# First lanes from the second group on, linear part on the last tile, VectorE scales the last two groups, a new order table

## Chip, cores and metric

The kernel runs on one core of a Trainium2 chip. The metric is the device time of one execution in microseconds. The kernel before takes 559.15 us (median of three runs, 559.07 to 559.81).

## The reference

Attention over 32 inducing points, twice, and then a feed-forward block with a PReLU:

```
B, N, C = 4, 12480, 128        # x
m = 32                         # inducing points
def mab(q, kv):
    a = softmax(scale * q @ kv.T)
    return a @ kv
h = mab(I, x)                  # per batch: 32 x 128
y = mab(x, h)                  # 12480 x 128 per batch
h1 = y @ w_in                  # 49920 x 2048
g = max(h1, 0) + alpha * min(h1, 0)
out = g @ w_out                # 49920 x 128, float32
```

## The kernel before

**What is computed per group.** Tokens are taken in groups of 512. A batch has 25 groups: six super-tiles of four groups and one last group of 192 tokens; groups are written (batch, number), so (0,0) to (3,24). The second attention has only 32 keys, so its product with `w_in` is folded into one small matrix per batch: hW = h @ w_in, 32 x 2048 (`h_weights`). Unnormalized softmax weights of a super-tile are computed (`b_scores`), go through DRAM (`e2d`) and come back four times below each other as `rep`, so that every 32-row strip of the tensor array finds a copy. A group then takes 16 *fills*: a matmul with 32 contraction rows (`hW` x `rep`) on one of the four 32-row strips, into a bank of PSUM, from where ACT or DVE writes relu to a `gt` tile in SBUF (`fill`, L596; ACT L614 or DVE L617). PReLU is relu times (1 - alpha) plus a linear part: the relu part goes through W1 = (1 - alpha) w_out, the linear part is one matmul with the small matrix hA (`linear`, one strip; `linear_whole` with a quarter of hA on all rows), which needs Amat (`w_amat`, 16 matmuls once) and `h_linear`. The sum of a group is transposed by DVE (`ot`, L664), scaled by the softmax denominators (`ob`, POOL, L667) and written out by four DMAs (`finish`, L653).

**Two ways to sum a group.** In the *whole* way the 16 gt tiles are contracted over all 128 rows, one matmul each (`whole`). In the *lanes* a gt tile is contracted in four strip matmuls of 32 rows. The first strip does its 16 for a group, hands the group to the second, and so on to the fourth; the four strips work on four different groups at once, each adding to its own bank, while fills go on whichever strip is free. A bank must not be written by two strips at a time: at a hand-over the next strip waits on a semaphore (`fence`), which is raised by a PE drain (`hand_over`, L966 to L974). Where the instruction before can carry the semaphore the drain vanishes in the built program; the others stand alone (L969, 19 of them before).

**The order.** `tokens` writes down PE's order by hand with a planner's clock: the lane loop chooses the next fill, piece, start, enter, warm or spare matmul by its model of when banks and tiles come free. `PLAN` has a letter for each laned group that sets four knobs (how hungry ACT and DVE must be, room, cost of a fill, whether to hand over at once). Other work (scores of later super-tiles, the next batch's first attention, transposes) is put into `tasks` at numbered steps; a step that touches PE in another shape is a pause, at which the lanes stop for a whole-array stage. The order of the engines' instructions is fixed (`pin`).

**Phases.** A prologue makes h of batch 0. Then SESSIONS (8) sessions do groups (0,0) and (0,1) the whole way: four fills, tasks, four whole matmuls of the session before. Then come the lanes for 92 groups, from a first `start` (step T0 = 9); the last group of each batch, and the groups (3,22) and (3,23), go the whole way, the last three in the tail. While strips 2 and 3 have nothing in the first lanes, *warm* matmuls on W1 go there (`fresh`), and *spare* ones at the end. The `gt` pool has KEPT = 62 tiles. `rep` tiles come from a pool of three; the part of the first super-tile that PE makes directly (`rep0`, L522) takes one of the three.

**DMA queues.** POOL's queue issues loads of x (`a_load`) and most output; SP's issues e2d, rep, rt, rdT and the transposes; the last four groups' outputs go by SP and ACT, and two of group (3,23) wait in `late` until the end (POOL, L688).

The lines that start a lane are these:

```
tile[0] = [queue.pop(0), [None] + list(range(KC))]
...
t = max(free_at[f], seen[ch][1] - 100 - SLOT)
```

None stands for the linear part.

Of the kernel before, what the change touches and what calls it, by code (L numbers as in the profile page):

```python
# [17 lines left out]
P = 128  # L18
NB = 4
GRP = P * NB  # L20
NQ = 4
# [3 lines left out]
TAIL = 2  # L25
AHEAD = 8
LAND = 8000
KEPT = 62
RDS = 4
# [8 lines left out]
PLAN = (  # L38
    "aaKKfGcyLqmADMamiiznjafamQcyaqcafqanqaxacmOaav"
    "AmnCamKeacfymraaJmRnAynqyauaNmmgadjmafycQazyAm"  # L40
)
# [3 lines left out]
def kernel(  # L45
# [476 lines left out]
    def b_scores_pe(st, q):  # L522
        if q == 0:
            st.rep0 = rep_pool.tile([P, NQ, GRP], bf16, name="rep", tag="rep")
        ps = bank()
        mm(ps[:], st.hT4[:], tokens_of(st, 0, q))
        pin(nc.scalar.activation(
            out=st.rep0[:, q, :].rearrange("p (t j i) -> p t j i", j=NB, i=32),
            in_=turned(ps[:], NB), func=EXP, scale=scale_of(st),
        ))  # L530
        drained(ps, "A", 490, 240)
        st.rep[q] = st.rep0[:, q, :]
# [120 lines left out]
    def finish(b, g):  # L653
        st = states[b]
        pp, nb, _ = shape_of(g)
        t = pp * nb
        acc = acc_of(b, g)
        s, q = divmod(g, NQ)
        rq = st.rden[s][:, :, :, q : q + 1]
        rbc = bass.AP(  # L660
            tensor=rq.tensor, offset=rq.offset, ap=[rq.ap[0], rq.ap[1], rq.ap[2], [0, 32]]
        )
        ot = ot_pool.tile([P, GRP], f32, name="ot", tag="ot")
        pin(nc.vector.transpose(out=ot[:, :t], in_=acc[:, :t]))  # L664
        drained(accs[b, g], "D", 74 + t * 1.04)
        ob = ob_pool.tile([P, GRP], f32, name="ob", tag="ob")
        pin(nc.gpsimd.tensor_tensor(  # L667
            out=ob[:, :t].rearrange("p (k m c) -> p k m c", k=nb, c=32),
            in0=ot[:, :t].rearrange("p (k m c) -> p k m c", k=nb, c=32),
            in1=rbc, op=MULT,  # L670
        ))
        t0 = b * N + s * SUP
        if s < NS:
            dst = out[t0 : t0 + SUP, :].rearrange(
                "(i b q) (a k) -> q a i b k", b=t // 32, q=NQ, k=32)[q]
        else:
            dst = out[t0 : t0 + REM, :].rearrange("(i b) (a k) -> a i b k", b=t // 32, k=32)
        ending = b == B - 1 and g >= NG - 4
        for a in range(4):
            eng = (nc.sync, nc.scalar)[a % 2] if ending and g >= NG - 3 else nc.sync if ending else nc.gpsimd  # L680
            src = ob[32 * a : 32 * a + 32, :t].rearrange("p (b k) -> p b k", k=32)
            if b == B - 1 and g == NG - 2 and a > 1:
                late.append((dst[a], src))
            else:
                pin(eng.dma_start(out=dst[a], in_=src))  # L685
        if b == B - 1 and g == NG - 1:
            for dst, src in late:
                pin(nc.gpsimd.dma_start(out=dst, in_=src))  # L688
        st.rep.pop(g)
# [132 lines left out]
    def tokens(st):  # L822
# [15 lines left out]
        tail = [y for y in direct[2:] if y[0] == B - 1]  # L838
        tail.sort()
# [3 lines left out]
        need = [ch for _, ch in sorted(need)]  # L843
        SESSIONS = 8
        T0 = SESSIONS + 1

# [13 lines left out]
        at(4, lambda: b_turn(st, 0))  # L860
        at(5, w_amat)
        at(6, lambda: h_linear(st))
        for b in range(B):
            base = T0 + (first[b, 0] if b else -2)
            for s in range(1, NS + 1):
                t = base + 4 * s - AHEAD - (b == 0 and s > 4) if b or s > 2 else 4 * s - 2
                nt = t + (5 if b == 0 and s == 2 else 3 if b == 0 and s == 4 else 4 if s < NS or b + 1 < B else 2)
# [4 lines left out]
            if b + 1 < B:  # L872
# [7 lines left out]
                else:  # L880
                    score = [T0 + k for k in (2, 4, 4, 6, 9, 11, 13)]
                    load = [0, 0, 5, SESSIONS, T0 + 2, T0 + 4, T0 + 6]
                    cross = [None, None, 6, T0 + 1, T0 + 4, T0 + 7, T0 + 8]
                    at(7, lambda: p_xpose(states[1], 0, 0))
                    at(SESSIONS, lambda: p_xpose(states[1], 0, 1))
                    at(T0 + 2, lambda: p_xpose(states[1], 1, 0))
                    at(T0 + 3, lambda: p_xpose(states[1], 1, 1))
                sums = [T0 + k for k in (4, 6, 6, 9, 11, 13, 14)] if n == 1 else [k + 4 for k in score]
                fs, fa = (t_scores, t_accum) if n == 1 else (a_scores, a_accum)
# [31 lines left out]
        for t in range(SESSIONS):  # L921
# [32 lines left out]
        assert len(plans) == len(laned)  # L954
        fresh = {f: bank() for f in (2, 3)}

# [19 lines left out]
        while queue or moving or owed or any(tile):  # L976
            best = []
            taken = {q for _, q, _ in moving} | {f + 1 for _, f in owed}
            for f in range(4):
                if tile[f]:  # L980
                    y, todo = tile[f]
                    if todo[0] is None:
                        best.append((free_at[f], 0, f, "linear"))
                    elif (*y, todo[0]) in seen:
                        t = max(free_at[f], seen[*y, todo[0]][1] - 100)
                        best.append((t, 1, f, "piece"))
                else:
# [4 lines left out]
                    if f == 0 and queue and lanes < LANES and (  # L992
# [3 lines left out]
                        if ch in seen:  # L996
                            t = max(free_at[f], seen[ch][1] - 100 - SLOT)
                            best.append((t, 2, f, "start"))
            if fillable():
                since = max(min(clk.free[i] for i in idle) - 40, landed.get(need[0][:2], 0))  # L1000
                hungry = min(clk.act, clk.dve) < clk.pe + hungry_at
                for f in range(4):
# [3 lines left out]
                    elif not tile[f]:  # L1006
                        best.append((t, 4 + (f in taken), f, "fill"))
            soon = min(max(x[0], clk.pe) for x in best) < clk.pe + 2 * SLOT
            for f in sorted(fresh):
# [7 lines left out]
            calm += [x for x in best if x[3] in ("warm", "spare")]  # L1017
            if owed and not best:
                hand_over()
                continue  # L1020
            if owed and not calm and at_once:
# [16 lines left out]
            if what == "start":  # L1038
# [11 lines left out]
                else:  # L1050
                    run_tasks(T0 + m)
                tile[0] = [queue.pop(0), [None] + list(range(KC))]
                continue
            if what == "enter":
                x = next(x for x in moving if x[1] == f)
                moving.remove(x)
                tile[f] = [x[0], list(range(KC))]
                gate[f] = fences[x[0], f]
# [16 lines left out]
            else:  # L1075
# [4 lines left out]
                else:  # L1080
# [5 lines left out]
                    if f == 3:  # L1086
                        seen.pop(ch)
                    if not todo:
                        tile[f] = None
                        if f < 3:  # L1090
                            owed.append((y, f))
                        flush()
            free_at[f] = clk.pe + SLOT
# [51 lines left out]
```

## Time and profile before

| | us |
|---|---|
| median of three runs | 559.15 |
| the profiled execution | 558.86 |
| its span, first to last instruction | 557.1 |
| first fills of the sessions | from 25.38 |
| lanes, with whole-array stages between | 41.66 to 541.68 |
| last three groups, whole | 541.68 to 550.59 |
| last output DMA issued on POOL | 552.27 |

The largest groups of instructions, with count, busy time, mean duration in ns of one and, after the second bar, idle time before them and what ended it:

```profile
L138 PE MATMUL bank<-gt,W 32*128 32x512 bf16 (+1 forms) x6013 | 482.9, 374 | 1.6 <-DVE gt L617 0.3
L614 ACT ACTIVATE gt<-bank 128x512 bf16<-128x512 f32 (+1 forms) x923 | 467.9, 620 | 14.3 <-PE bank L138 10.2
L617 DVE TENSOR_SCALAR gt<-bank 128x512 bf16<-128x512 f32 (+1 forms) x645 | 403.7, 676 | 19.9 <-PE bank L138 16.4
L667 POOL TENSOR_TENSOR ob<-ot,rdT 128x512 f32<-128x512 f32 (+1 forms) x100 | 111.0, 1110 | 93.5 <-DVE ot L664 83.7
```

Busy times of matmuls overlap: four strips work at once, so a mean of 374 ns each is not 374 ns of time. ACT's and DVE's instructions follow each other more closely than their means say: 467.9 us for 923 are 0.51 us each, 403.7 for 645 are 0.63. Granted TensorE clock was 0.998 over the span.

### The profile page before, as it was taken

The numbers are of one execution on the slowest core, as the hardware profiler recorded it, in microseconds if no ns is written. First come the engines' busy times: TensorE is split into PE (matmuls) and PEld (weight loads), VectorE is DVE, ScalarE is ACT, GpSimd is POOL, SyncE is SP. The second block draws the span as 40 slices with busy tenths as digits, with TensorE's granted clock in tenths as the row PEclk, the third lists the DMA queues.
The fourth block names the chain that finished last, engine by engine and source line by source line (L and its number), as shares of the span: only waits on it lengthen the run. The fifth ranks groups of instructions, "written<-read, shape, count | busy, mean of one in ns | idle before, by whom it ended". The sixth has DMA issues, their size and how long they took to land.

```text
span 557.1 us, 21434 instructions
## 1 busy us (share of the span) xinstructions
PE 538.6 (97%) x8890; PEld 293.1 (53%) x8894; DVE 497.3 (89%) x858; ACT 503.8 (90%) x1008; POOL 411.4 (74%) x602
## 2 busy tenths in 40 slices
PE   4999999999999999999999999999999999999995
PEld 4645555555455555544555556554465554454642
DVE  3689999989999999999998999999998999999981
ACT  2479999999989999999999999999999999999980
POOL 6556466967898978878698878665668859767683
PEclk9999999999999999999999999999999999999999
DMA  9976999645999998687577996333334334333224
GB/s 196 230 136 142 134 192 176 132 94 89 151 199 165 176 144 164 148 120 150 102 131 131 169 170 140 64 93 88 75 81 112 73 81 118 65 94 65 47 62 75
DMA packets 110209, 69.25 MB, mean 124 GB/s; under 512 B 78800, under 2 KB 100672, under 8 KB 110112
## 3 DMA queue, kind: packets, MB, share of 16 engines
q0 software_dynamic: 23344, 38.66, 37.6%
q1 hardware_dynamic: 84624, 28.46, 26.3%
q8 instruction: 69, 1.13, 0.9%
q10 hardware_dynamic: 2144, 0.77, 0.5%
q14 instruction: 28, 0.23, 0.2%
HBM read 41.00 MB, written 28.95 MB: 126 GB/s over the span
## 4 chain that ended last, share of the span: by engine, by line
PE 31%; issue 27%; PEld 25%; POOL 8%; DMA 4%; ACT 3%; DVE 1%; PEldq 1%; POOLq 0%; DVEq 0%
PE bank L138 31%; PEld L138 25%; POOL out_dram L685 5%; DMA xn<-in_x_dram 3%; POOL ob L667 3%; ACT gt L614 2%; PEldq L969 1%; PE bank L226 1%; DMA out_dram<-ob 1%; DVE gt L617 1%; DVE hW L313 0%; POOL xn L180 0%; DVE ot L664 0%; DMA rt<-rd 0%; PEld bank L138 0%
## 5 line engine op out<-in xcount | busy, mean ns | idle before, releaser
L138 PE MATMUL bank<-gt,W 32*128 32x512 bf16 (+1 forms) x6013 | 482.9, 374 | 1.6 <-DVE gt L617 0.3
L614 ACT ACTIVATE gt<-bank 128x512 bf16<-128x512 f32 (+1 forms) x923 | 467.9, 620 | 14.3 <-PE bank L138 10.2
L617 DVE TENSOR_SCALAR gt<-bank 128x512 bf16<-128x512 f32 (+1 forms) x645 | 403.7, 676 | 19.9 <-PE bank L138 16.4
L138 PE MATMUL bank<-rep,hW 32*128 32x512 bf16 (+1 forms) x1600 | 417.9, 368 | 2.0 <-DVE hW L313 0.3
L138 PEld LDWEIGHTS <-W 32*128 32x128 bf16 (+1 forms) x6109 | 229.1, 92 | 188.0 <-issue 117.2
L685 POOL DMA_DIRECT2D out_dram<-ob x384 | 247.0, 673 | 36.9 <-POOL ob L667 27.8
L667 POOL TENSOR_TENSOR ob<-ot,rdT 128x512 f32<-128x512 f32 (+1 forms) x100 | 111.0, 1110 | 93.5 <-DVE ot L664 83.7
L138 PEld LDWEIGHTS <-hW 32*128 32x128 bf16 x1600 | 135.6, 91 | 31.3 <-issue 15.1
L664 DVE STREAM_TRANSPOSE ot<-bank 128x512 f32<-128x512 f32 (+1 forms) x100 | 69.7, 697 | 16.3 <-PE bank L138 15.0
L180 POOL DMA_DIRECT2D xn<-in_x_dram x70 | 40.4, 656 | 3.6 <-DMA xn<-in_x_dram 2.4
L138 PE MATMUL bank<-rep,hA 32*128 32x512 bf16 x94 | 35.0, 376 | 0.3 <-DVE hW L313 0.2
L232 DVE COPY xT<-bank 128x1024 bf16<-128x1024 bf16 (+1 forms) x16 | 10.8, 672 | 5.1 <-PE bank L226 4.9
L138 PE MATMUL bank<-W 32*128 32x512 bf16 x93 | 13.8, 376 | 0.0
L253 ACT ACTIVATE e1t<-bank 128x256 bf16<-128x256 f32 (+1 forms) x13 | 4.8, 372 | 9.7 <-PE bank L138 9.5
L138 PEld LDWEIGHTS <-hA 32*128 32x128 bf16 x94 | 8.5, 91 | 7.3 <-issue 4.8
L226 PE MATMUL bank<-ident,xn 128*128 128x128 bf16 x128 | 11.3, 242 | 0.9 <-DVE xn L786 0.9
L138 PE MATMUL bank<-xT,hT 128*32 128x512 bf16 (+1 forms) x98 | 10.4, 389 | 0.6 <-ACT gt L614 0.4
L498 ACT ACTIVATE e<-bank,rs 128x512 bf16<-128x512 f32 x12 | 8.4, 699 | 2.5 <-PE bank L138 2.3
L226 PEld LDWEIGHTS <-xn 128*128 128x128 bf16 x128 | 8.7, 109 | 2.2 <-DVE xn L786 1.0
L498 ACT ACTIVATE e<-bank 128x512 bf16<-128x512 f32 x12 | 7.4, 616 | 2.4 <-PE bank L138 2.4
L138 PE MATMUL bank<-IT,xT 128*128 128x32 bf16 x192 | 8.0, 179 | 0.2
L138 PEld LDWEIGHTS <-hT 128*32 128x32 bf16 (+1 forms) x122 | 5.0, 93 | 5.8 <-issue 4.0
(103 smaller groups left out, 144.4 us busy)
## 6 DMA issues: line engine op xcount, KB each, us to landing
out_dram<-ob POOLq DMA_DIRECT2D x374, 64.0 KB, 2.9
rep<-e2d SPq DMA_DIRECT2D x92, 128.0 KB, 3.3
xn<-in_x_dram POOLq DMA_DIRECT2D x48, 128.0 KB, 5.5
xn<-in_x_dram POOLq DMA_DIRECT2D x22, 256.0 KB, 6.9
e2d<-e SPq DMA_DIRECT2D x24, 128.0 KB, 3.1
rdT<-rt SPq DMA_DIRECT2D x96, 8.0 KB, 2.4
w_out_f<-in_moe_w_out_dram POOLq DMA_DIRECT2D x4, 256.0 KB, 11.2
xs<-in_x_dram SPq DMA_DIRECT2D x1, 512.0 KB, 4.8
```

Of the source, the lines that this page charges most:

```text
L138: return pin(nc.tensor.matmul(o, lhsT, rhs, start=start, stop=stop, **kw))
L180: pin(nc.gpsimd.dma_start(out=xn[:, i * w : (i + 1) * w, :], in_=src[:, i * w : (i + 1) * w, :]))
L226: pin(nc.tensor.transpose(tp[:, k * P : (k + 1) * P], xn[:, q, j * C : (j + 1) * C], ident[:]))
L232: pin(nc.vector.tensor_copy(out=dst, in_=tp[:, :w]))
L253: pin(nc.scalar.activation(out=e1t[:pp, :nb, :].rearrange("p k m -> p (k m)"), in_=ps[:pp, : nb * M], func=EXP, scale=scale,))
L498: pin(nc.scalar.activation(out=e2[:].rearrange("p (t j i) -> p t j i", j=n, i=32), in_=turned(ps[:pp, :w], n), func=EXP, scale=scale_of(st ...
L614: pin(nc.scalar.activation(out=gt[:, :w], in_=ps[:, :w], func=RELU))
L617: pin(nc.vector.tensor_relu(gt[:, :w], ps[:, :w]))
L664: pin(nc.vector.transpose(out=ot[:, :t], in_=acc[:, :t]))
L667: pin(nc.gpsimd.tensor_tensor(out=ob[:, :t].rearrange("p (k m c) -> p k m c", k=nb, c=32), in0=ot[:, :t].rearrange("p (k m c) -> p k m c", ...
L685: pin(eng.dma_start(out=dst[a], in_=src))
L969: pin(nc.tensor.drain(fusable=True)).then_inc(fence, 1)
```

## The change

Groups: SESSIONS goes from 8 to 4, and only (0,0) is summed the whole way at the start; (0,1) becomes the first laned group, 93 in all. Amat, h_linear and the linear part of (0,0) become stages at the first three steps of the lanes; the scores of super-tile 2 come at step 4 in place of 6, and the steps of batch 1's first attention move with T0 (5 in place of 9) and by one or two more. The linear part stands behind the 16 pieces on strip 3 in place of before them on strip 0, and is offered only once hA is there. Warm matmuls are only for strip 3. `rep0` gets its own tile of two groups; `gt` has two tiles less. The last two groups' scaling is on DVE. PLAN is another table, with one letter more.

```
-KEPT = 62
+KEPT = 60
 PLAN = (
-    "aaKKfGcyLqmADMamiiznjafamQcyaqcafqanqaxacmOaav"
-    "AmnCamKeacfymraaJmRnAynqyauaNmmgadjmafycQazyAm"
+    "aaLCMLqymRymyimmKyalcavyVacyvMdiamfyafGcjamDcy"
+    "xyKnKymeqazGaaneialaMjaMFaMjccjommQamlcclccKya"
+    "a"
 )
...
-            st.rep0 = rep_pool.tile([P, NQ, GRP], bf16, name="rep", tag="rep")
+            st.rep0 = const.tile([P, 2, GRP], bf16, name="rep0")
...
-        pin(nc.gpsimd.tensor_tensor(
+        eng = nc.vector if b == B - 1 and g >= NG - 2 else nc.gpsimd
+        pin(eng.tensor_tensor(
...
-        direct = every[:2] + [(b, NG - 1) for b in range(B)] + every[-1 - TAIL : -1]
+        direct = every[:1] + [(b, NG - 1) for b in range(B)] + every[-1 - TAIL : -1]
...
-        SESSIONS = 8
+        SESSIONS = 4
...
-        at(5, w_amat)
-        at(6, lambda: h_linear(st))
+        at(T0, w_amat)
+        at(T0 + 1, lambda: h_linear(st))
+        at(T0 + 2, lambda: (linear_whole(0, 0), flush()))
...
-            base = T0 + (first[b, 0] if b else -2)
+            base = T0 + (first[b, 0] if b else -1)
...
-                t = base + 4 * s - AHEAD - (b == 0 and s > 4) if b or s > 2 else 4 * s - 2
+                t = base + 4 * s - AHEAD - (b == 0 and s > 4) if b or s > 2 else 2 * s
...
-                    score = [T0 + k for k in (2, 4, 4, 6, 9, 11, 13)]
-                    load = [0, 0, 5, SESSIONS, T0 + 2, T0 + 4, T0 + 6]
-                    cross = [None, None, 6, T0 + 1, T0 + 4, T0 + 7, T0 + 8]
+                    score = [T0 + k for k in (3, 5, 5, 7, 10, 12, 14)]
+                    load = [0, 0, SESSIONS, T0 + 1, T0 + 3, T0 + 5, T0 + 7]
+                    cross = [None, None, T0 + 1, T0 + 2, T0 + 5, T0 + 8, T0 + 9]
...
-        for f in range(2):
-            linear(0, f, f)
...
-        finish(*held.pop(0))
         run_tasks(SESSIONS)
-        flush()
...
-        fresh = {f: bank() for f in (2, 3)}
+        fresh = {3: bank()}
...
-                        best.append((free_at[f], 0, f, "linear"))
+                        if hasattr(states[y[0]], "hA"):
+                            best.append((free_at[f], 0, f, "linear"))
...
-                            t = max(free_at[f], seen[ch][1] - 100 - SLOT)
+                            t = max(free_at[f], seen[ch][1] - 100)
...
-                tile[0] = [queue.pop(0), [None] + list(range(KC))]
+                tile[0] = [queue.pop(0), list(range(KC))]
...
-                tile[f] = [x[0], list(range(KC))]
+                tile[f] = [x[0], list(range(KC)) + [None] * (f == 3)]
```

In the built programs the change moves these counts: whole matmuls on W1 128 to 112, strip matmuls on W1 and gt 5888 to 5952, warm and spare matmuls 93 to 61, standalone drains 19 to 26, evictions by ACT 923 to 927 (of these 18 of 384 columns in place of 20), by DVE 645 to 641.

More of the change, by code (lines that the diff above doesn't have):

```diff
@@ L837, in tokens @@
                 wholes[c + 1].append((b, NG - 1, u))
-        tail = [y for y in direct[2:] if y[0] == B - 1]
+        tail = [y for y in direct[1:] if y[0] == B - 1]
         tail.sort()
@@ L880, in tokens @@
                 else:
-                    score = [T0 + k for k in (2, 4, 4, 6, 9, 11, 13)]
-                    load = [0, 0, 5, SESSIONS, T0 + 2, T0 + 4, T0 + 6]
-                    cross = [None, None, 6, T0 + 1, T0 + 4, T0 + 7, T0 + 8]
[L884 to L888, printed above, removed]
+                    score = [T0 + k for k in (3, 5, 5, 7, 10, 12, 14)]
+                    load = [0, 0, SESSIONS, T0 + 1, T0 + 3, T0 + 5, T0 + 7]
+                    cross = [None, None, T0 + 1, T0 + 2, T0 + 5, T0 + 8, T0 + 9]
+                    at(T0 + 1, lambda: p_xpose(states[1], 0, 0))
+                    at(T0 + 2, lambda: p_xpose(states[1], 0, 1))
+                    at(T0 + 3, lambda: p_xpose(states[1], 1, 0))
+                    at(T0 + 4, lambda: p_xpose(states[1], 1, 1))
+                sums = [T0 + k for k in (5, 7, 7, 10, 12, 14, 15)] if n == 1 else [k + 4 for k in score]
                 fs, fa = (t_scores, t_accum) if n == 1 else (a_scores, a_accum)
@@ L1007, in tokens @@
                         best.append((t, 4 + (f in taken), f, "fill"))
+            if owed and not best:
+                hand_over()
+                continue
             soon = min(max(x[0], clk.pe) for x in best) < clk.pe + 2 * SLOT
@@ L1017, in tokens @@
             calm += [x for x in best if x[3] in ("warm", "spare")]
-            if owed and not best:
-                hand_over()
-                continue
             if owed and not calm and at_once:
@@ L1087, in tokens @@
                         seen.pop(ch)
[L1088 to L1092, printed above, removed]
+                if not todo:
+                    tile[f] = None
+                    if f < 3:
+                        owed.append((y, f))
+                    flush()
             free_at[f] = clk.pe + SLOT
```

## Prediction

> **What bounds the kernel now.** I read the page first, then the windows by stage, then PE's timeline where the lanes begin and every engine's timeline at the end.
>
> ```profile
> span 557.1 us, 21434 instructions
> PE 538.6 (97%) x8890; PEld 293.1 (53%) x8894; DVE 497.3 (89%) x858; ACT 503.8 (90%) x1008; POOL 411.4 (74%) x602
> ...
> PE 31%; issue 27%; PEld 25%; POOL 8%; DMA 4%; ACT 3%; DVE 1%; PEldq 1%; POOLq 0%; DVEq 0%
> ```
>
> The chain of waits is 83% TensorE in its three forms. ACT and DVE are no bystanders, though, as the windows show (per stage: PE, PEld, DVE, ACT, POOL busy, clock, DMA share, GB/s):
>
> ```profile
> 33.73:41.66 7.93, 7.44 (x74) 3.83 (x72) 6.69 (x15) 5.03 (x9) 1.59 (x4) 1.00 1.01 170
> 41.66:75.79 34.13, 34.13 (x575) 18.20 (x573) 31.54 (x53) 32.26 (x65) 20.54 (x29) 1.00 0.88 154
> 75.79:300.00 224.21, 222.53 (x3819) 119.69 (x3819) 208.92 (x364) 215.83 (x437) 178.87 (x258) 1.00 0.80 142
> ...
> 541.68:550.60 8.92, 8.86 (x52) 4.68 (x51) 2.15 (x3) 0.00 (x0) 4.69 (x7) 1.00 0.49 88
> ```
>
> In the lanes (row three) ACT is 96% and DVE 93% busy: TensorE and the two evicting engines are nearly in balance, so neither can gain much there alone. The first row is the last part of the sessions: there ACT is 63% and DVE 84% busy. That is the one stage before the tail in which all three engines have slack, and the change takes it out.
>
> PE's timeline there (start, duration, tiles, count):
>
> ```profile
> 32.66 0.81 PE L138 MATMUL bank<-gt,W 128*128 128x512 bf16 x3 [0.16 <-issue]
> 33.40 0.39 PE L138 MATMUL bank<-rep,hW 32*128 32x512 bf16 x4
> 33.73 1.07 PE L138 MATMUL bank<-AW,winT 128*128 128x128 bf16 x16
> 34.63 1.03 PE L138 MATMUL bank<-gt,W 128*128 128x512 bf16 x4
> 35.59 0.39 PE L138 MATMUL bank<-rep,hW 32*128 32x512 bf16 x4
> ...
> 41.66 0.39 PE L138 MATMUL bank<-rep,hW 32*128 32x512 bf16 x2
> 41.67 0.39 PE L138 MATMUL bank<-W 32*128 32x512 bf16 x2
> ```
>
> Four fills, then four whole matmuls, with switches between: from 33.40 on, 8.26 us for 16 fills. The lanes begin at 41.66.
>
> The unit of the rest: a *round* is one 32-row matmul of 512 columns on a strip; in a stretch between two whole-array stages the fullest strip counts the rounds. I counted each stretch's matmuls in the order of the built program and took its time from PE's timeline. The 33 stretches from 41.66 to 541.68 have 1965 rounds in 464.2 us: **0.2362 us a round**. By work (all strips' matmuls over four: 1899) it is 0.2444. The whole-array stages between take the other 35.8 us. A whole matmul costs 0.216 (the tail's run of 15 takes 3.40 us, the last alone about 0.38).
>
> **The change part by part.** *Counts that cancel.* Group (0,1) leaves the whole array: 16 whole matmuls fewer (3.46 us), 64 strip matmuls more. 32 warm or spare matmuls go (93 to 61). Evictions stay at 1568; a net 4 move from DVE to ACT. I cost these through the rounds below, not twice.
>
> *The start.* The built program after the change keeps fills and whole matmuls as they are up to the fifth block of fills at 32.11. Then come the whole matmuls (to 33.40), the scores of super-tile 2 moved up (0.33 from start to next start, as at 36.66 to 36.99 here), four fills (0.33), and the Amat product, which the first lane waits for (0.90, from 33.73 to 34.63). Lanes start at 33.40 + 0.33 + 0.33 + 0.90 and a switch of some 0.15: **35.1**. What the cut sessions held moves into the lanes: up to the stage with the rest of batch 1's accumulations, which opens at 75.79 before, the new order has 145 rounds in place of 130, and five whole-array stages in place of three. Rounds at this region's own pace: the 130 took 31.1 us, 0.239 each, so 145 take 34.7. Stages from their parts: the stage at 51.92 took 1.46 (pick, scores, transposes, IT products); pick and transposes alone are 0.64, with Amat's product 0.71; the one at 57.96 (transposes) took 0.55, with the whole linear 0.77; the other three 1.28, 0.64 and 1.03; sum 4.4. So the common point comes at 35.1 + 34.7 + 4.4 = 74.2 against 75.79, with 142 fills issued against 140 and one piece fewer. Two added drains (none before) may take 0.1 of it. **-1.5 us.** Bounds: at the quickest stretch's 0.221 a round the 145 cost 2.6 less (-4.1); at 0.245, the slowest here, 0.8 more, and if evictions hold the first lane by a further 1 us, the end is +0.3.
>
> *Common point to the end of lanes.* The same stages; 1839 rounds against 1835, by work 1777.0 against 1775.75. Standalone drains (L969): 24 more against 19, which is 5 more. By work +1.25 x 0.2444 = +0.3; by rounds +0.9. A drain lasts 0.55 us (median of 19) against 0.24 for the round it displaces, so 5 cost up to 1.6 if nothing else was late; a fit over the 33 stretches gives 0.06 to 0.12 each, because evictions catch up meanwhile and the next rounds run closer. I take **+0.3**, by work, since three engines share the bound here; the other end is +0.9 + 1.6 = +2.5. The fit misses a stretch by 0.28 us, over 29 stretches 1.5 us: so it may also be -1.2.
>
> *Linear part on the last tile.* 92 strip matmuls change from strip 0 to strip 3, one becomes a whole one (0.22 in place of 0.06); contained in the rounds. A group's transposition starts one matmul (0.22) later, and its bank was taken one later too. Nothing is queued behind but the next group's.
>
> *Queues and buffers.* SP: the e2d and rep transfers of super-tile 2 (5 DMAs) pass the rt, xTr and rdT transfers of super-tile 1; POOL: two xn loads pass the first ob. SP would hold rt by a landing of e2d, 3.1 us median; rdT's readers are covered, since POOL waits for DVE's ot in 83.7 us of its idle time and for rdT once (9.7). Two gt buffers less: the program's stock peaks at 59 in place of 61 and lies at 45 to 58 for most of the run. Nothing for either; without that cover a fill waits one eviction, 0.6.
>
> *The end.*
>
> ```profile
> 549.33 0.72 DVE L664 STREAM_TRANSPOSE ot<-bank 128x512 f32<-128x512 f32 x1 [2.95 <-PE bank L138]
> 550.13 1.55 POOL L667 TENSOR_TENSOR ob<-ot,rdT 128x512 f32<-128x512 f32 x2 [2.59 <-DVE ot L664]
> 550.70 0.38 DVE L664 STREAM_TRANSPOSE ot<-bank 128x192 f32<-128x192 f32 x1 [0.66 <-PE bank L138]
> 551.62 1.29 POOL L688 DMA_DIRECT2D out_dram<-ob  x2
> ```
>
> DVE has no two-tensor row of 128x512 in SBUF. Nearest: its TENSOR_SCALAR of 128x512, 0.68; its TENSOR_TENSOR of 128x128, 0.29; POOL's 1.08 as upper end. With 0.68, ob of group 23 is done at 550.8 (551.2 on POOL), the last ot waits 0.1 behind it on DVE and ends at 551.2, the last ob (192 wide, about 0.37) at 551.6, as before. SP, which issued from 551.23, starts at 550.85, waits for the last ob and issues two at 551.7 in place of 551.9. **-0.2** (-0.4 to +0.4, with POOL's duration).
>
> Sum: -1.5 + 0.3 - 0.2 = **-1.4** against the profiled execution: 558.86 to 557.5 (span 557.1 to 555.7). That execution lies 0.3 under the median of 559.15, so 557.8 in the median's terms.
>
> A rule that speaks against the change stands in the Trainium skill, "TensorE: Matmul & The Clock Gate", section "Measured speedup vs the span model": four row tiles were measured at 3.07 times one, not 4. By it group (0,1) would cost 16 x 0.216 x 4/3.07 = 4.5 us as strips, an estimate, against 3.8 at 0.2362 a round; the sum would be -0.7. Here the trace differs: 333 strip matmuls in the 19.92 us from 144.16 are 59.8 ns each, 3.6 times one. The 558.5 that the rule gives shares the chance of rival (1).
>
> **The rivals.** *(1) The start gives little.* Lanes open at 35.1 but the first lane, alone on strip 0, waits for its gt: 16 pieces in line need 3.5 us, and only 4 of their gt are evicted by then. For: DVE and ACT evict one in 0.63 and 0.51, so 12 more take 3.4 us, no faster. Against: from 41.66 to 75.79 the two together idled 4.5 us, 0.13 for each us. The start then gives 0.4: -0.4 + 0.3 - 0.2 = -0.3, 558.9. The same comes out if the first strips run at some 0.247 a round for another reason; 0.05 of its chance is for that.
>
> *(2) Slower: the drains.* PE stands still 0.55 in each, 26 times in place of 19. If no eviction is behind at that moment, the 0.31 over a round is lost every time. Place: L969's rows in mid-lanes, where at 169.64 the next full set of starts came 0.4 after the drain. Price: 7 x 0.31 = 2.2 and 0.9 for the rounds: -1.5 + 3.1 - 0.2 = +1.4, 560.5. It decides from about 0.27 a drain on, where the sum passes +1.1. Against: the fit's 0.06 to 0.12.
>
> *(3) Faster than forecast.* The evictors set the time. From 33.73 to 41.66 they idle 4.1 engine-us; at 0.13 an us they would idle 1.0: 3.1/2 = 1.6 on the clock. With 0.2 at the end and a rest of -1.0, within its bounds, for an order that keeps them fed: -2.8, 556.4. For: their 93 to 96%.
>
> **How the numbers follow.** Forecast (557.8, own range 557.0 to 558.4) 0.36; (1) 0.25; (2) 0.19; (3) 0.20. One measurement tells 0.2%, 1.1 us, from no change: under 558.0 is faster, over 560.3 slower. About three quarters of the forecast's case, with all of (3), is faster: 0.47; the rest of it and (1): 0.34; (2): 0.19. Range 555.4 to 560.6: from (3) a further 1 us down for its bounds, and up to (2).
>
> **What would show it.** First lane pieces near 35.1; batch 1's last accumulations opening at 74.2; 26 DRAIN rows, with the stretches around them at 0.236 a round; lanes ending 1.2 earlier, near 540.5; the tail's whole stretch unchanged at 8.9; a DVE ob row of 0.68. It is wrong if stretches with two drains run over 0.25 a round, if the common point comes after 75.5, or if the end after the last matmul grows.

## The result, and the profile after

The changed kernel took **561.04 us** (median of 9 runs, 560.29 to 562.83) beside 559.08 for the kernel before on the same chip: ratio 1.0035, 95% interval 1.0025 to 1.0046. It is slower by 2.0 us, where 1.4 less was forecast, and lies 0.4 above the range. The profiled execution took 560.92 with a span of 558.8, against 558.86 and 557.1.

The page's busy times and the chain's shares by engine:

```profile
PE 539.6 (97%) x8906; PEld 285.1 (51%) x8910; DVE 495.3 (89%) x856; ACT 504.0 (90%) x1012; POOL 409.6 (73%) x600
...
PE 32%; issue 27%; PEld 26%; POOL 5%; DMA 4%; DVE 3%; ACT 1%; PEldq 1%; SPq 0%; POOLq 0%; DVEq 0%
```

Little in it tells the two kernels apart: TensorE's three forms are 85% of the chain in place of 83%. The windows by stage (per stage: length; PE, PEld, DVE, ACT and POOL busy; clock, DMA share, GB/s) and PE's timeline where the lanes open say more:

```profile
35.73:74.93 39.20, 38.71 (x636) 20.61 (x635) 36.42 (x63) 37.64 (x76) 18.43 (x26) 1.00 0.89 159
...
544.25:553.17 8.92, 8.87 (x51) 4.68 (x51) 2.67 (x4) 0.00 (x0) 4.08 (x5) 1.00 0.50 90
```

```profile
34.07 0.40 PE L139 MATMUL bank<-xT,hT 128*32 128x512 bf16 x4
34.40 0.40 PE L139 MATMUL bank<-rep,hW 32*128 32x512 bf16 x4
34.73 1.07 PE L139 MATMUL bank<-AW,winT 128*128 128x128 bf16 x16
35.73 0.39 PE L139 MATMUL bank<-rep,hW 32*128 32x512 bf16 x1
```

The order at the lanes' opening is the one that was read from the built program. The tail's whole stretch is 8.92 in both. The end:

```profile
551.90 0.72 DVE L665 STREAM_TRANSPOSE ot<-bank 128x512 f32<-128x512 f32 x1 [2.98 <-PE bank L139]
552.65 0.69 DVE L669 TENSOR_TENSOR ob<-ot,rdT 128x512 f32<-128x512 f32 x1
553.27 0.38 DVE L665 STREAM_TRANSPOSE ot<-bank 128x192 f32<-128x192 f32 x1
553.64 1.29 POOL L690 DMA_DIRECT2D out_dram<-ob  x2 [3.56 <-DVE ob L669]
553.69 0.36 DVE L669 TENSOR_TENSOR ob<-ot,rdT 128x192 f32<-128x192 f32 x1
```

DVE's ob takes 0.69 and 0.36 (0.68 and 0.37 were estimated). The last matmul ends at 553.17; SP and ACT issue their first transfers behind it 0.20 later (0.63 before), and POOL its two from 0.47 on (1.03 before).

The difference of the two profiled executions, laid out along the program (us):

| stretch | before | after | change | forecast |
|---|---|---|---|---|
| span's start to the first fills | 25.38 | 26.37 | +0.99 | 0 |
| first fills to the common point | 50.41 | 48.56 | -1.85 | -1.5 |
| common point to the end of the lanes | 465.89 | 469.32 | **+3.43** | +0.3 |
| the tail's whole stretch | 8.92 | 8.92 | 0 | 0 |
| last matmul to the span's end | 6.49 | 5.67 | -0.82 | -0.2 |
| outside the span | 1.76 | 2.12 | +0.36 | 0 |

The rows add up to 2.1, the whole difference. What was meant to gain did, and a little more; most of the loss lies in the third row, where the forecast saw nearly the same work. By the phases between batch 1's, 2's and 3's pauses that row reads (a *lane stretch* is the time between two whole-array stages; 0.2338 us is about the pace of both kernels net of drains, worked out below):

| phase ends at | change | rounds | drains | lane stretches less 0.2338 a round |
|---|---|---|---|---|
| batch 1's pause (164.1, 164.4) | +1.18 | +3 | +2 | +0.57 |
| batch 2's (294.3, 294.4) | -0.16 | -5.75 | +2 | +1.23 |
| batch 3's (420.8, 422.7) | +1.75 | +8.5 | +1 | -0.74 |
| end of the lanes (541.7, 544.3) | +0.66 | -4 | 0 | +1.68 |

Of the sum, 1.75 rounds are 0.4 (this count has stretches cut by whole-array stages alone, and gives 1.75 where the forecast's gave 4) and the whole-array stages 0.3; 2.7 is left for five more drains and for the order itself.

### The profile page after: what moved, and what is told of

Its sections match the earlier page's. It is cut to its first block, busy times and chain, and to the rows that moved or that the text cites. A ratio compares the mean times of both kernels' runs of the same rounds, so it can differ in the third digit from the quotient of the medians.

```text
span 558.8 us, 21541 instructions
## 1 busy us (share of the span) xinstructions
PE 539.6 (97%) x8906; PEld 285.1 (51%) x8910; DVE 495.3 (89%) x856; ACT 504.0 (90%) x1012; POOL 409.6 (73%) x600
## 4 chain that ended last, share of the span: by engine, by line
PE 32%; issue 27%; PEld 26%; POOL 5%; DMA 4%; DVE 3%; ACT 1%; PEldq 1%; SPq 0%; POOLq 0%; DVEq 0%
PE bank L139 31%; PEld L139 25%; POOL out_dram L687 3%; DVE gt L618 2%; POOL ob L669 1%; DMA xTr<-xnr 1%; PE bank L227 1%; ACT gt L615 1%; DMA xT<-xn 1%; PEldq L968 1%; DMA ind_f<-in_inducing_dram 1%; DMA rep<-e2d 1%; DVE ot L665 1%; POOL xn L181 0%; PEld L227 0%
## 5 line engine op out<-in xcount | busy, mean ns | idle before, releaser
L139 PE MATMUL bank<-gt,W 32*128 32x512 bf16 (+2 forms) x6062 | 484.2, 374 | 2.6 <-PEq L968 0.6
L139 PEld LDWEIGHTS <-W 32*128 32x128 bf16 (+1 forms) x6125 | 220.6, 92 | 192.3 <-issue 121.6
L669 POOL TENSOR_TENSOR ob<-ot,rdT 128x512 f32<-128x512 f32 (+1 forms) x98 | 108.3, 1105 | 92.3 <-DVE ot L665 80.2
L139 PE MATMUL bank<-W 32*128 32x512 bf16 x61 | 12.1, 375 | 0.0
```

The source lines that it names most:

```text
L139: return pin(nc.tensor.matmul(o, lhsT, rhs, start=start, stop=stop, **kw))
L669: pin(eng.tensor_tensor(out=ob[:, :t].rearrange("p (k m c) -> p k m c", k=nb, c=32), in0=ot[:, :t].rearrange("p (k m c) -> p k m c", k=nb, ...
```

## The experiments

Ratios are to the kernel before, run beside on the same chip.

### The change taken apart

*The changed kernel once more.*

> The changed kernel once more, for a second profile. In the first one TensorE stood still for 1.1 us at 18.6 us, in the prologue, whose instructions are the same in both kernels. If that stall belongs to the program, it is there again and the first fills start near 26.4 us; if it is of that one execution, they start near 25.4 us and the median stays about 2 us over the kernel before all the same.

561.26, ratio 1.0046 (1.0029 to 1.0063). Its profile is worth more than its time: all 33 stretches lasted within 0.02 us of what they lasted in the first one. So a stretch's length belongs to TensorE's order, and two programs with one order can be compared stretch by stretch, to a few hundredths, but for a few restless stretches that are named below.

*Hand-over at once switched off in all 93 letters:*

```
-    "aaLCMLqymRymyimmKyalcavyVacyvMdiamfyafGcjamDcy"
...
+    "aaKCMKqymQymyimmKyakcauyUacyuMciameyaeGciamCcy"
...
```

> The changed kernel with the knob for handing over at once off in all 93 letters of the table: no standalone drain is left of 26, rounds go from 1981 to 1995. If time follows the rounds alone (0.236 us each): +3.2 us over the changed kernel. If each drain costs the 0.31 us by which it is longer than a round: -8.1 + 3.2 = -4.8 us. If about 0.1 us each, as the fit over the stretches of before gave: +0.6 us.

572.65, ratio 1.0241 (1.0228 to 1.0254): 26 drains less, 14 rounds more, and 11.4 us slower than after. Its lane stretches run at 0.2425 a round.

*The old table, with an "a" ahead for the added lane:*

```
-    "aaLCMLqymRymyimmKyalcavyVacyvMdiamfyafGcjamDcy"
...
+    "aaaKKfGcyLqmADMamiiznjafamQcyaqcafqanqaxacmOaa"
...
```

> The changed kernel with the table of before, an 'a' put ahead for the group that is new in the lanes: 2001 rounds for 1981, 6 standalone drains for 26. If the new table is what made it slower, this is faster than the changed kernel by 2 us or more. By rounds alone +4.8 us; with 0.31 us a drain -1.4 us; with 0.1 us a drain +2.8 us.

576.86, ratio 1.0320 (1.0307 to 1.0334). So the new table isn't what makes the changed kernel slow; with the old one it is 16 us slower.

*The linear part first again, on strip 0, where its operand is there; the new table kept:*

```
-                tile[0] = [queue.pop(0), list(range(KC))]
+                y = queue.pop(0)
+                if not hasattr(states[y[0]], "hA"):
+                    latelin.add(y)
+                tile[0] = [y, [None] * (y not in latelin) + list(range(KC))]
...
-                tile[f] = [x[0], list(range(KC)) + [None] * (f == 3)]
+                tile[f] = [x[0], list(range(KC)) + [None] * (f == 3 and x[0] in latelin)]
```

> The changed kernel with the linear part first on strip 0 again, where hA is there; the table stays. The planner then writes another order: 1974 rounds for 1981, 12 standalone drains for 26. By rounds alone -1.6 us; with 0.1 us a drain -3.0 us; with 0.31 us a drain -5.9 us. If the place of the linear part were worth something by itself, it would be slower.

570.64, ratio 1.0202 (1.0189 to 1.0215), with 12 drains and 1974 rounds. All three variants opened their lanes at 35.44 or 35.45 (after at 35.73 and, once more, 35.46) and lost 9 to 16 us behind that. No account by rounds and drains gives that: with the drain's price found below, all three should have been faster than after. Each altered the planner's input under a table that was fitted to another; that became the theory for the rest.

The last variant shows one more thing. SP loads a rep tile anew when TensorE has read it for the last time, and the linear part reads rep. What SP's `rep<-e2d` waited for TensorE (us in total, times, longest) in before, in after and in this variant:

```profile
SPq L516 <- PE bank L138: 6.3, 18, 0.5
SPq L517 <- PE bank L139: 113.7, 21, 10.0
SPq L517 <- PE bank L139: 6.1, 15, 1.1
```

It is 110 to 119 us in the changed kernel's other profiles, above and below, whatever their table, and 4 to 8 in all of before's: putting the linear part on the last strip holds SP's queue up by some 107 us. What stands behind in that queue comes later, the transposing DMA of x among it. Before, and after, with the matmuls that need that `xT` (the loads of rep ahead of it were issued from 325.19 and 329.42):

```profile
327.18 4.31 SPq L194 DMA_TRANSPOSE xT<-xn  x1
336.83 0.60 PE L138 MATMUL bank<-xT,IT 128*32 128x512 bf16 x8
```

```profile
331.34 1.98 SPq L195 DMA_TRANSPOSE xT<-xn  x1
336.69 0.40 PE L139 MATMUL bank<-xT,IT 128*32 128x512 bf16 x4 [0.19 <-DMA xT<-xn]
```

The transposition lands at 334.33 before and at 336.64 after, where TensorE already waits. This whole-array stage takes 1.17 us in all seven profiles with before's order (1.17 to 1.32 in the three variants above), and 1.55, 1.48, 2.34, 3.62 and 4.13 in the five with after's. Two of those three variants have the linear part last and SP held as long (115 and 119 us), and the stage takes 1.20 and 1.17 there: whether the hold reaches TensorE depends on the order too.

### The price of a drain

*The kernel before, with 21 drains added at lanes' starts, the order of everything else kept:*

```
                 else:
                     run_tasks(T0 + m)
+                    pin(nc.tensor.drain(fusable=True)).then_inc(spare, 1)
```

> The kernel before with TensorE's order unchanged and 21 standalone drains added, one at each lane's start that is not at a whole-array stage (40 in the lanes in place of 19). Theory that drains cost the difference (0.31 each, rival 2): 21 x 0.31 = +6.5 us, ratio 1.0116. Theory of the forecast (0.06 to 0.12 each, evictions catch up meanwhile): +1.3 to +2.5, ratio 1.002 to 1.0045. If two drains in one stretch are what hurts, the stretches that now hold two or more lose 0.5 each and those with one 0.1 to 0.2.

567.91, ratio 1.0143 (1.0123 to 1.0164). A stretch of before with two drains, then the same here with one more (windows; PE, PEld, DVE, ACT, POOL busy):

```profile
251.49:273.92 22.43, 22.08 (x365) 11.54 (x361) 21.02 (x36) 21.64 (x44) 18.64 (x27) 1.00 0.76 146
```

```profile
254.72:277.47 22.75, 22.24 (x365) 11.30 (x361) 21.00 (x36) 21.66 (x44) 18.57 (x27) 1.00 0.74 144
```

The same matmuls and evictions take 0.32 longer; the stretch that was at 296.73, with two drains added to its one, takes 0.45 longer. Every stretch without an added drain kept its length to 0.02, but for the last (+0.13), that at 482.44 (+0.07) and those at 65.17 and 77.49, which moved in an unchanged run too (below). The one at 401.02 got 1.57 longer with two drains, but took 19.77 to 20.88 in four executions of unchanged order. Without the last and those at 65.17, 77.49 and 401.02, 19 drains cost 6.0 us: **0.32 each**. The forecast's 0.06 to 0.12 falls; rival (2)'s 0.31 holds. (Expectations further on say 0.42: that is this profile's whole loss in the lanes over the 21, restless stretches included.) By stretch it is 0.22 to 0.51 a drain; stretches that got two or three paid 0.22 to 0.29 for each, so that drains don't make each other dearer.

*The same in the changed kernel, 11 drains added:*

> The changed kernel with TensorE's order unchanged and 11 drains added at lanes' starts (37 in the lanes in place of 26). At the 0.42 us of the kernel before: +4.6 us against after, ratio to before about 1.0125. At the 0.06 to 0.12 of the forecast: +0.7 to +1.3, ratio 1.006. If a second drain in a stretch costs more than the first, +0.5 each, +5.5.

566.67, ratio 1.0132 (1.0104 to 1.0159). In the stretches that have them the 11 cost 3.25 us, 0.30 each. Another 4.2 us of this profile are the wait for `xT` at 338 (2.78) and the stretch behind it (1.6 longer).

*The kernel before with four of its own drains gone.* A hand-over's mark can ride on the last piece (a strip matmul on a gt tile) unless that matmul already signals a released buffer. A one-column matmul that adds zeros takes that signal, where another group stands open on its strip and can carry it; 11 such matmuls were added:

```
+        def carry(y, f):
+            c = (f + 1) % 4
+            rows = slice(32 * f, 32 * f + 32)
+            mm(
+                accs[y][:, 0:1], W1[rows, 0, :], pick[rows, c : c + 1],
+                start=False, stop=False, skip_group_check=True,
+            )
...
             if owed and not calm and at_once:
+                on = [q for q in range(4) if tile[q] and q not in gate and tile[q][0] in begun]
                 hand_over()
+                if on:
+                    carry(tile[on[-1]][0], on[-1])
```

> The kernel before with TensorE's order kept, but four of its 19 standalone drains in the lanes gone: where a group that needs no hand-over stands open on a strip, a one-column matmul that adds zeros to it takes the release count that kept the drain from riding on the last piece, and the hand-over's mark goes on that piece. If a drain costs the 0.42 us that the added ones cost, the lanes get 4 x 0.42 = 1.7 us shorter (ratio 0.997), all of it in the stretches that lose a drain, the others within 0.02 us. If only an added drain costs (one that the planner had not reckoned with) and those of the table are free, nothing moves (within 0.3 us).

559.03, ratio 0.9998 (0.9988 to 1.0008): not told from no change by the time. The profile is finer. One of the four stretches (two drains before, one now) and its count of drains (x is the count; ns min/median/max):

```profile
251.60:273.71 22.11, 21.91 (x365) 11.63 (x361) 21.01 (x36) 21.58 (x44) 18.59 (x27) 1.00 0.79 148
```

```profile
L977 PEldq DRAIN  x15: 423/550/858, 107.3 to 485.6; - x15
```

It lasts 22.11 in place of 22.43; the four lose 0.13, 0.32, 0.32 and 0.16. The others keep their length to 0.04, but for two restless ones (-0.14 at 77.49, +0.12 at 401.02). So drains that the planner had reckoned with cost too: 0.23 each.

*Three drains taken from the changed kernel,* by switching the hand-over at once off in three letters of the table after which the order falls back into its old course:

```
-    "xyKnKymeqazGaaneialaMjaMFaMjccjommQamlcclccKya"
+    "xyKnKymeqazGaaneiakaMiaMEaMjccjommQamlcclccKya"
```

> The changed kernel with the hand-over-at-once knob off in three letters of its table (65, 68 and 71): 23 drains in the lanes in place of 26, 1981 rounds as before, and TensorE's order the same again some instructions after each of the three places. If a drain costs its 0.55 less the round it displaces, 0.2 to 0.32: 0.6 to 1.0 us less than after, in the three stretches that lose one. If the later hand-over costs as much as the drain, nothing moves or those stretches grow, by up to 1 us in all.

562.76, ratio 1.0067 (1.0044 to 1.0089): not faster than after. The first of the two stretches that lose the three drains, after and here:

```profile
380.56:402.74 22.18, 21.97 (x363) 11.32 (x363) 21.00 (x37) 21.45 (x44) 15.13 (x21) 1.00 0.38 88
```

```profile
385.31:408.23 22.92, 22.91 (x371) 11.42 (x371) 21.69 (x38) 22.33 (x46) 15.06 (x21) 1.00 0.38 88
```

Two drains fewer, yet three rounds more (94 for 91) and 0.74 longer; with the following stretch (one drain and three rounds fewer) the pair takes 42.17 in place of 41.51. At 0.3 a drain it should have taken 0.9 less; handing over later cost 1.6. For these three a drain has its price, but leaving it out by waiting costs more. That the kernel without any is 11 us slower goes the same way; but its whole order differs, and no run says how much of the 11 us this is. The rest of this profile's loss is two stops, of 2.67 at 168 (last section) and of 2.27 at 339, the wait for `xT`.

### What a table is worth

*The kernel before with hand-over at once off everywhere* (each letter's last knob, as above; a guard is moved up so that the planner finds a next step, which alone leaves the order as it was):

> The kernel before with the hand-over-at-once knob off in all its letters: 1 drain in the lanes in place of 19, 1972.75 rounds in place of 1964.25, another order. If rounds and drains are the whole account: 8.5 x 0.236 - 18 x 0.42 = -5.6 us, ratio 0.990. If an order that the table was not fitted to costs some 10 us whatever it is, as in the changed kernel (+11.4 over after): +8 to +12, ratio 1.016 to 1.022, with the pace of the stretches without a drain up from 0.235 to over 0.24.

574.23, ratio 1.0272 (1.0255 to 1.0289).

*The kernel before with two gt buffers fewer* (and the same guard):

```
-KEPT = 62
+KEPT = 60
```

> The kernel before with its own table and two gt buffers fewer, as the change has it: the planner answers with another order from the middle on (1966.5 rounds, 8 drains). If rounds and drains are the whole account: +0.5 - 11 x 0.42 = -4.1 us, ratio 0.993. If a table loses its worth with any change of what it was fitted to: +5 to +12, ratio 1.01 to 1.02. Two buffers alone, without the order, are worth nothing by the forecast.

576.87, ratio 1.0318 (1.0299 to 1.0336).

*The kernel before with one letter changed* (and the guard):

```
-    "aaKKfGcyLqmADMamiiznjafamQcyaqcafqanqaxacmOaav"
+    "aaKKfGcyLqmADMamiiznjafamQcyaqcaeqanqaxacmOaav"
```

> The kernel before with one letter of its table changed (the 33rd, hand-over-at-once off): the planner gives another order from the lanes' first third to the end, with 1960 rounds (4 fewer) and 13 drains (6 fewer). If rounds and drains are the whole account: -4.25 x 0.234 - 6 x 0.3 = -2.8 us, ratio 0.995. If most of the table's worth is that it was fitted on the chip to the exact order it gives, one letter costs 5 to 12 us (ratio 1.01 to 1.02), beginning at the first stretch that differs.

567.03, ratio 1.0134 (1.0119 to 1.0149). By rounds, and 0.3 a drain, the three should have gained 3.4, 2.8 and 2.8 us; they lost 15.0, 17.6 and 7.6. The last lane stretch, in before and with the one letter:

```profile
504.24:541.68 37.44, 37.29 (x596) 20.74 (x597) 34.70 (x59) 35.37 (x71) 27.26 (x37) 1.00 0.28 57
```

```profile
512.94:554.16 41.22, 40.80 (x630) 21.87 (x630) 34.25 (x58) 34.97 (x71) 29.47 (x41) 1.00 0.29 57
```

Both have 160 rounds, and the evictors do the same work in it (DVE 34.3 to 34.7, ACT 35.0 to 35.4); of the 34 matmuls more, 24 are spare ones and ten are pieces. It takes 3.8 us longer, half of the median's loss, 300 us behind the letter; that pieces and fills there come in an order in which somebody always waits is argued, and not taken apart by a run. (The profiled execution, 571.34, was the slowest of its five, with a stop of 1.95 us at 172.) In the changed kernel the same stretch takes 38.55 for 161 rounds. So six orders under a table made for another lost 8 to 18 us. That the loss is the table's misfit, and not what each edit does by itself, is argued from six unlike edits; a table fitted anew to one of them would show it. By that reading the change's parts can't be priced one at a time under a table made for another order, and both kernels have a table that fits. Net of 0.3 a drain, before runs at 0.2334 us a round behind the common point, and after at 0.2340. The orders with a foreign table run at 0.2425 to 0.245 over all, with few drains or none.

### Buffers, prologue and end

*The kernel before with the first rep tile in a buffer of its own:*

```
-            st.rep0 = rep_pool.tile([P, NQ, GRP], bf16, name="rep", tag="rep")
+            st.rep0 = const.tile([P, 2, GRP], bf16, name="rep0")
```

> The kernel before with the first super-tile's rep tile in a buffer of its own, as the change has it; TensorE's order is that of before. Two theories of the 0.7 to 1.0 us by which the first fills come later after the change, though the instructions ahead of them are the same: if it is the place of the buffers in memory (or the rotation of the rep buffers), the first fills move here from 25.38 to about 26.1 and the whole is 0.7 slower (ratio 1.0012); if it comes from elsewhere (the order of the queues' later work, the fetching of another instruction stream), they stay at 25.38 and the time within 0.2 of before.

560.27, ratio 1.0005 (0.9995 to 1.0016); first fills at 25.46. So this buffer isn't what moves the first fills.

*The kernel before once more:*

> The kernel before once more, unchanged, for its profile: its first was the only one of this order that had the first fills at 25.38. If the prologue's 0.7 us belongs to the execution and not to the change, the first fills come at 26.1 here, as in four of the five other programs with this order, and the lanes' sum lies between 464.2 and 466.3 us with every difference in one or two stretches. If it belongs to the change, they come at 25.4.

559.43, ratio 1.0000 (0.9992 to 1.0009), first fills at **26.04**. The same program came at 25.38 and at 26.04, and after at 26.37 and 26.09, so that most of this row of the table above is an execution's and not the change's. 29 of its 31 stretches lasted within 0.02 of the first profile's; that at 65.17 went from 10.62 to 10.72 and that at 77.49, with a stop of 0.65 in it, from 15.80 to 16.66. Against this execution the third row of the table is +2.5, not +3.4. In the four profiles of this order with all its drains and no more, that row's length is 465.9 (the first), 466.8 (this one), 467.2 and 468.0; in the two profiles of after it is 469.3 and 469.2. So the third row is worth 1.2 to 3.4, by the execution that one compares with. The first profile's time (558.86) is near its median; this one's, 560.23, was the slowest of eleven.

*The kernel before with the last two groups' ob products on VectorE, and the changed kernel with them back on GpSimd:*

```
-        pin(nc.gpsimd.tensor_tensor(
+        eng = nc.vector if b == B - 1 and g >= NG - 2 else nc.gpsimd
+        pin(eng.tensor_tensor(
```

> The kernel before with one thing of the change alone: the last two groups' ob products on VectorE. TensorE's order is that of before. If the end's gain is its own (after: 0.87 us less from the last matmul to the span's end), the span shortens by 0.5 to 0.9 us, 558.3 or so, ratio 0.9985. If the gain of the end belongs to something else of the change (another arrival of the last groups), it is 0.2 as forecast, or none. Nothing before the last matmul should move: the first fills at 25.38, the lanes at 41.66, their end at 541.68.

> The changed kernel with the last two groups' ob products back on GpSimd; TensorE's order is that of after. If VectorE gave the 0.87 us after the last matmul, this is 0.5 to 0.9 us slower than after (562.1, ratio to before about 1.006), all of it behind the last matmul; if not, within 0.2 of it.

559.63, ratio 0.9992 (0.9983 to 1.0001), and 563.71, ratio 1.0066 (1.0042 to 1.0091). From the last matmul to the span's end: 6.02 in place of 6.49 in before's order, 5.99 in place of 5.67 in after's. VectorE is worth 0.3 to 0.5 there, and SP's and ACT's last issues come 0.40 and 0.43 sooner with it. The rest of the 0.82 lies behind the last output's landing: from there to the span's end before takes 1.53, after 1.21, after with GpSimd 1.20. It isn't the new order's, since the three variants of after with other orders end 5.63 to 5.71 behind the last matmul too; whose it is, no run shows. The second's time is more than that above after's: its profiled execution, 561.84 with a wait of 0.98 for `xT` in it, was the fastest of six, which go up to 566.28, and what the others hold no trace shows.

*Both gains in the kernel before: VectorE at the end, and the four carried drains.*

> The kernel before with what the runs showed to gain at its own order: the last two groups' ob products on VectorE, and four of the 19 drains carried by one-column matmuls. Worked out from the stretches: 0.9 less in the lanes and 0.7 to 0.9 behind the last matmul, so 1.7 us, ratio 0.997. If the two medians of those runs (0.9992 and 0.9998) are nearer the truth: 0.999.

**558.15, ratio 0.9977 (0.9968 to 0.9985)**: faster than both kernels. Its end:

```profile
549.30 0.72 DVE L664 STREAM_TRANSPOSE ot<-bank 128x512 f32<-128x512 f32 x1 [2.95 <-PE bank L138]
550.05 0.69 DVE L668 TENSOR_TENSOR ob<-ot,rdT 128x512 f32<-128x512 f32 x1
```

The transposition still ends 0.72 after its start, and the first ob follows 0.03 behind it. The measured gain of 1.3 us is about what the stretches gave: 0.9 in the lanes and 0.5 at the end.

## Why the prediction was wrong, point by point

- **The start: right.** The lanes opened 9.36 behind the first fills, where 35.1 against 25.38 said 9.7; the common point came 1.85 earlier in place of 1.5. The 15 more rounds took 3.54, 0.236 each, with their two drains in it; the stages took 1.5 more (1.4 in the sum). Rival (1), a first lane that starves, falls: the two evictors idled 4.3 engine-us between the lanes' opening and the common point, 0.11 for each us (0.13 before), and the added rounds kept the pace.
- **Common point to the end of the lanes: the step that failed.** The sum put nothing in for drains, on the ground that "a fit over the 33 stretches gives 0.06 to 0.12 each, because evictions catch up meanwhile". The runs show 0.2 to 0.3 a drain in a given order, in both kernels, added or removed. Five are 1.5 at 0.3. The likely reason is that stretches with a drain are also those in which a group was handed over at once, so that the fit read price and benefit as one; the three drains taken from after fit this, though no run tests the fit itself. The rounds, 1.75 more, took 0.4, and "The same stages" 0.3 more in all; the one at 335 that waits for `xT` took 0.4 more by itself (1.55 for 1.17). These parts are 2.2, in the middle of the 1.2 to 3.4 that the executions give for this row. In the first two profiles 1.2 is left over; it goes up and down by the phases without regard to drains (the last column above), and no run puts it on one place. The evictors' idle time behind the common point, 54.2 engine-us against 44.1, goes the same way; no run shows it as a cause.
- **The bound that was left open was the wrong one.** The sum gave +2.5 as the other end for rounds and drains, and the range was cut at rival (2), 560.5. The price in that rival, 0.31, lies within the measured 0.23 to 0.32, and its forecast came nearest. That its number came so near is in part luck, since it had no term for the prologue's 0.99 or the 0.36 outside the span. The parts that are priced (start -1.85, drains, rounds and stages +2.2, end -0.8) would make the change 0.5 faster; the 2.0 by which it is slower holds also the prologue, the time outside the span and the 1.2 above, none of which a run ascribes to a part of the change. So the drains' price is shown, and what makes up the rest of the medians' difference stays open. The stage that waits for `xT`, longer by 0.3 to 3.0 us in the five profiles of after's order, is a candidate.
- **The end: right in sign, too small.** 0.82 in place of 0.2. The durations were right, and VectorE alone gave 0.3 to 0.5; the sum had SP's issues come 0.2 sooner, and they came 0.4 sooner. The remainder lies behind the last landing and was not in it.
- **Linear part and queues: put at nothing, wrongly.** "Nothing is queued behind but the next group's" overlooks the rep tile, which the linear part now reads three strips later. SP's loads of rep wait 113.7 us for TensorE in place of 6.3, and the transposition behind them makes TensorE wait: 0.19 in the first profile of after, up to 2.78 in others.
- **Buffers: not to be had singly.** With 60 gt buffers after has the same pace as before with 62, net of drains. The run with KEPT = 60 alone shows what the forecast didn't weigh: the number steers the planner, and another order under a foreign table cost 17.6 us.
- **The rule on four row tiles** ("TensorE: Matmul & The Clock Gate", "Measured speedup vs the span model", in the Trainium skill) would have given -0.7 for the sum. The trace doesn't bear it out: 323 strip matmuls in the 19.38 us from 145.02 of after are 60.0 ns each, again 3.6 times one, and the start, where group (0,1) went to strips, gained more than forecast.

Of the signs named beforehand: lane pieces at 35.73 (35.1, with a prologue 0.99 later), common point at 74.93 (74.2), 26 DRAIN rows, ob 0.69, tail 8.92. Stretches with two drains ran at 0.242 to 0.245, under the 0.25 that was named as the alarm; that alarm was set too far off, since 0.3 in 20 us is only 0.004 a round.

## What to carry to other kernels

Price a stall by adding it to, or taking it from, an otherwise unchanged order; a regression over stretches of one kernel mixes the stall's cost with what it buys. Where a planner with a fitted table writes the order, compare fitted with fitted: an edit run under the other kernel's table loses 8 to 18 us here, whatever the edit. Where an order repeats to a few hundredths, compare stretch by stretch: 0.2 us can be read there that the whole time, with its scatter of 1 to 2 us, hides. And where a read moves to a later step, ask which buffer it frees, and what stands in the queue behind that buffer's next load.

## What the runs showed of the hardware

A drain of TensorE lasts 0.53 to 0.55 us here (medians in after and before; 0.65 for the 21 added ones) and costs 0.2 to 0.3 net on average, 0.13 to 0.51 by stretch. And TensorE stands still for 0.6 to 2.7 us in some executions, with nothing awaited that the profile shows, weight loads included:

```profile
168.08 0.38 PE L139 MATMUL bank<-gt,W 32*128 32x512 bf16 x1
171.12 0.39 PE L139 MATMUL bank<-gt,W 32*128 32x512 bf16 x3 [2.67 <-issue]
```

That is the kernel with three letters changed; the same order passed here without a stop in after. The kernel before with one letter changed had one of 1.95 at 172 and one of 0.92 at 81, and the kernel before, once more and with 21 drains added, one of 0.65 and 0.64 at 81. Neither profile on which the comparison rests has one. A late transfer of instructions is a candidate, and no run tested it. By the traces' DMA packets each of these stops ends 2.5 to 3.0 us after such a transfer (queue q8) began, which for the longest was at 168.3, where after has it at 164.3, and for the second at 171.1, where the kernel before once more has it at 167.9. Such stops, and the waits for `xT`, may be why some medians above lie over what the stretches say; only the profiled executions can be looked at.
